# Even and odd columns apart in a two-layer Winograd convolution block, with positions 1 and 3 by columns in three chunks of layer two, and another issue order

## The chip, the cores and the metric

The kernel runs on one core of one Trainium2 chip. The metric is the device time of one execution in microseconds (us); less is better. The median before is that of three runs.

## What is computed

The kernel is a residual block of a diffusion model on two images of 512 channels and 64 x 64 points, in bf16. Each of two layers normalizes in four groups of 128 channels, applies SiLU, and convolves 3 x 3. An embedding is added between the layers, and the input at the end.

```python
B, C, HW, E = 2, 512, 64, 1152
def reference(x, t_emb, g1, be1, w1, w_emb, g2, be2, w2):
    ...
    h = conv3(_silu(gn(x, g1, be1)), w1)
    emb = _silu(t_emb) @ w_emb
    h = h + emb.reshape(B, C, 1, 1)
    h = conv3(_silu(gn(h, g2, be2)), w2)
    return x + h
```

## The kernel before

**Tiling.** The 512 channels are four blocks of 128 partitions: `ct` counts those of the input, `ot` those of the output. Each image is cut into two chunks of 32 rows, so each layer has four chunks (`chunks`, index `idx`). A chunk's rows form eight tiles (`TR`) of four output rows (`TH`).

**Winograd over rows.** Four output rows of three taps need six products in place of twelve, the positions 0 to 5. `u_blocks` turns the weights (transposed by TensorE, L392, and copied out of PSUM, L505) into six weight sets U; `v_block` turns the activated rows into six row sets V. A position is then a plain one-dimensional convolution over columns: three taps `kx`, each a product of 128 x 128 weights with 8 rows x 64 columns = 512 columns, read from a row of 66 elements (`WP`, with one zero at each end) at offset 0, 1 or 2. For four `ct` that makes 12 products, accumulated in one half of an accumulator of two PSUM banks; there are three accumulators (`next_acc`). All these products are issued by `groups` (L655); `row_pair` does two positions.

**The same over columns.** Where `is_col` holds (layer one's chunks 1 to 3, all of layer two), positions 0 and 5 use a second such step over pairs of columns: four products of 256 columns (`c` = 0 to 3) in place of three of 512, in `col_pair`. Products 0 and 3 read every second element of a difference, products 1 and 2 a sum and a difference that lie side by side; the last lines of `make_v` write these. In the last two chunks of layer two positions 1 and 3 go by columns as well: `u_more` makes their weights, `v_more_split` (chunk three) and `v_more` (chunk four) their V, `more_cols` and `more_pair` their products and sums.

**Sums.** `one_set` does one `ot` of one chunk: its accumulators are read by ScalarE (`act`, L353), added on VectorE (`tt`, L323; `stt`, L336; `ts`, L328) and written into an output buffer `yst`. Column results land with stride two, at even and odd columns. In layer one the result goes to `h_scr` in DRAM; in layer two the input is added by a DMA on GpSimd's queue, and a DMA writes the output. `final_set` does the very last `ot`.

**Buffers.** `v_block` loads rows of x or h into `src[i]`, SiLU writes them to `a_tmp[i]` with zeroed edges (GpSimd), and `make_v` works through `vt` into V; `i` alternates between 0 and 1. `Vbuf` holds V of two chunks: that of chunk `idx + 2` overwrites that of chunk `idx` when its products are done.

**Start.** All of the first image is loaded; `first_stats` gets the sums of squares by products of each 128 x 128 block with itself (L955), and plain sums by products with ones (L969) or by ScalarE and VectorE (`SUMS`). `norm` makes scale and shift from them on TensorE, VectorE and GpSimd.

**Order.** Everything is a node of `_Plan` with an engine, an estimated cost, and what it reads and writes. `issue` makes the order of each engine's instructions in a model of the core; it tries 100 variations (`PASSES`), each with noise on all priorities, and keeps the best model time. That order is written out as it is; nothing is reordered behind it.

Of the kernel before, what the change touches and what calls it, by code (L numbers as in the profile page):

```python
# [12 lines left out]
ALU = mybir.AluOpType  # L13
# [11 lines left out]
class _Plan:  # L25
# [5 lines left out]
    PASSES = 100  # L31
    JUSTIFY = 2
# [110 lines left out]
    def issue(self):  # L143
# [23 lines left out]
        rng = random.Random(1)  # L167
        late = backward([-d for d in due])
        best = None
        for k in range(self.PASSES):  # L170
            if best is None:
                trial = late
            else:
                noise = self.NOISE * math.exp(rng.gauss(0.0, 1.0))
                trial = [t + noise * rng.gauss(0.0, 1.0) for t in best[1]]
            found = None
            for r in range(self.JUSTIFY + 1):
                order, start, span = forward(trial)
                if found is None or span < found[0]:
                    found = (span, trial, order, start)  # L180
                if r < self.JUSTIFY:
                    trial = backward([-b - c for b, c in zip(start, self.cost)])
            if best is None or found[0] <= best[0]:
                best = found
            self.spans = getattr(self, "spans", []) + [best[0]]
        _, _, order, start = best
# [6 lines left out]
def kernel(  # L193
# [39 lines left out]
    DVE_SUMS = (1,)  # L233
    COL0 = (1, 2, 3)
# [15 lines left out]
    SUMS = (0, 3)  # L250
# [30 lines left out]
    gparm = mb[0:4 * CT, 0, 0, 0:P]  # L281
# [118 lines left out]
    def norm(layer, b, c0, n, me, ps=None, quick=False):  # L400
# [5 lines left out]
        def mm():  # L406
# [5 lines left out]
        plan.add("DVE", 0.1, lambda: nc.vector.tensor_copy(out=tot[:], in_=ps if ps is not None else bank.get()[:]),  # L412
                 tok if ps is None else [ps], [tot[:]])
# [11 lines left out]
        quick = quick or (layer, b) == (1, B - 1)  # L425
        two(nvar[:], mu, mu, ALU.mult, quick)
        two(nvar[:], nvar[:], ex, ALU.add, quick)
        if quick:
            ts(nvar[:], nvar[:], 0.0, op=ALU.min, c2=-1.0, op1=ALU.mult)
        else:  # L430
# [6 lines left out]
             cost=0.7)  # L437
# [3 lines left out]
        two(nb, mu, sc, ALU.mult, quick)  # L441
        two(nb, nb, b_, ALU.add, quick)
# [90 lines left out]
    more_buf = lambda ct: (a_tmp + src)[ct]  # L533

    def v_more(V, X):
        rows = lambda kx, st: view(V, kx, [[2 * NI, 2], [WP, TR], [st, W // st]])
        dst = lambda o, n: view(X, o, [[n * TR, 2], [n, TR], [1, n]])
        tt(dst(0, W), rows(0, 1), rows(2, 1), ALU.subtract)
        tt(dst(4 * NC, W // 2), rows(1, 2), rows(2, 2), ALU.add)
        tt(dst(6 * NC, W // 2), rows(2, 2), rows(1, 2), ALU.subtract)  # L540

    spare = lambda ct: (stage + [g1t])[ct]

    def v_more_split(V, at, D):
        rows = lambda kx, st: view(at, kx, [[NI, 2], [WP, TR], [st, W // st]])
        tt(view(D, 0, [[W * TR, 2], [W, TR], [1, W]]), rows(0, 1), rows(2, 1), ALU.subtract)
        dst = lambda i: view(V, i * 2 * NI, [[NC, 2], [W // 2, TR], [1, W // 2]])
        tt(dst(0), rows(1, 2), rows(2, 2), ALU.add)
        tt(dst(1), rows(2, 2), rows(1, 2), ALU.subtract)

    def rhs_more_split(V, D, j, c):
        if c in (0, 3):
            return view(D, j * 2 * NC + (1 if c == 3 else 0), [[W, TR], [2, W // 2]])
        return view(V, (c - 1) * 2 * NI + j * NC, [[1, NC]])

# [3 lines left out]
    def rhs_row(V, pos, kx, col):  # L559
        i = pos - 1 if col else pos  # L560
        return view(V, i * NI + kx, [[WP, TR], [1, W]])

    def rhs_col(V, j, c, o=4 * NI):
        if c in (0, 3):
            return view(V, o + j * 2 * NC + (1 if c == 3 else 0), [[W, TR], [2, W // 2]])
        return view(V, o + (4 if c == 1 else 6) * NC + j * NC, [[1, NC]])

    def silu_rows(layer, b, ch, ct, res, at):
# [3 lines left out]
        for edge, r in ((ch == 0, 0), (ch == NCH - 1, CR + 1)):  # L572
            if edge:
                pool(lambda r=r: nc.gpsimd.memset(rows[:, r, 1:W + 1], 0.0), [], [rows[:, r, 1:W + 1]], cost=0.2)  # L574
        act(rows[:, lo - r0:hi - r0, 1:W + 1], res[:, lo * W:hi * W].rearrange("p (r w) -> p r w", w=W)
            if res.shape[1] == HW else res.rearrange("p (r w) -> p r w", w=W),
            func=ACT.Silu, bias=nb_all[layer, b][:, ct:ct + 1], scale=sc_all[layer, b][:, ct:ct + 1])

    def make_v(V, at, rs, col, on_act, split=False):
# [25 lines left out]
        if split:  # L605
# [4 lines left out]
        tt(view(V, o, [[W, 2 * TR], [1, W]]), view(vt_, vo, [[WP, 2 * TR], [1, W]]),  # L610
           view(vt_, vo + 2, [[WP, 2 * TR], [1, W]]), ALU.subtract)
        odd = view(vt_, vo + 1, [[WP, 2 * TR], [2, W // 2]])
        evn = view(vt_, vo + 2, [[WP, 2 * TR], [2, W // 2]])
        tt(view(V, o + 4 * NC, [[W // 2, 2 * TR], [1, W // 2]]), odd, evn, ALU.add)
        tt(view(V, o + 6 * NC, [[W // 2, 2 * TR], [1, W // 2]]), evn, odd, ALU.subtract)

    def v_block(layer, b, ch, ct, V, res=None, rs=None, on_act=(False, True, True)):
        at = a_tmp[count["v"] % 2]
        k = src[count["v"] % 2]
# [9 lines left out]
        split = layer == 1 and b * NCH + ch == len(chunks) - 2  # L629
        make_v(V, at, rs if rs is not None else k, is_col(layer, b, ch), (layer == 1,) + on_act[1:], split)  # L630
        if split:
            v_more_split(V, at, spare(ct))
# [14 lines left out]
    def groups(pos_rhs, accs, gid, lead=0.0):  # L647
        done = {}
        for key, ap, lhs, rhs_, cost in pos_rhs:
            clock["t"] += cost  # L650

            def emit(key=key, ap=ap, lhs=lhs, rhs_=rhs_):
                for l, r in zip(lhs, rhs_):
                    k = done.get(key, 0)
                    nc.tensor.matmul(ap, lhsT=l, rhs=r, start=k == 0, stop=k == total[key] - 1)  # L655
                    done[key] = k + 1
            plan.add("PE", cost, emit, list(lhs) + list(rhs_), [ap], group=("g", gid), lat=0.17, due=clock["t"], lead=lead)
# [8 lines left out]
    def row_pair(pair, U, V, col, gid, split):  # L666
        a = next_acc()
        todo = []
        for i, pos in enumerate(pair):
            for ct in range(CT):  # L670
                taps = [(u_tap(U[ct], pos, kx), rhs_row(V[ct], pos, kx, col)) for kx in range(NKX)]
                todo.append((i, a[:, i], [t[0] for t in taps], [t[1] for t in taps], 0.218 * NKX))
# [3 lines left out]
    def col_pair(cc, U, V, gid, lead=0.0, js=(0, 1)):  # L676
        a = next_acc()
        a4 = a[:].rearrange("p j (k n) -> p j k n", k=2)
        todo = []
        for j in js:  # L680
            for k, c in enumerate(cc):
                pairs = [(u_col(U[ct], j, c), rhs_col(V[ct], j, c)) for ct in range(CT)]
                todo.append(((j, k), a4[:, j, k], [t[0] for t in pairs], [t[1] for t in pairs], 0.11 * CT))
# [3 lines left out]
    def more_cols(U, V, gid):  # L687
        def cols(cc):
            a = next_acc()
            a4 = a[:].rearrange("p j (k n) -> p j k n", k=2)  # L690
            todo = []
            for j in range(2):
                for k, c in enumerate(cc):
                    pairs = [(u_col_more(U[ct], j, c), rhs_more_split(V[ct], spare(ct), j, c)) for ct in range(CT)]
                    todo.append(((j, k), a4[:, j, k], [t[0] for t in pairs], [t[1] for t in pairs], 0.11 * CT))
            groups(todo, a, (gid, "more", cc))
            return a4
        act(mb[:].rearrange("p k j n -> p j k n"), cols((1, 2)), scale=0.5 * KAPPA)
        tt(sd[:, 0], mb[:, 0], mb[:, 1], ALU.add)
        tt(sd[:, 1], mb[:, 0], mb[:, 1], ALU.subtract)  # L700
        aa = cols((0, 3))
        for k, f in ((0, KAPPA), (1, -KAPPA)):
            stt(view(m1, k, [[NFREE, 2], [2, NC]]), aa[:, :, k], f, sd[:, k], ALU.mult, ALU.add)

    def more_set(j, U, gid):
        a = next_acc()
        todo = []
        for k, c in enumerate((0, 3, 1, 2)):
            pairs = [(u_col_more(U[ct], j, c), rhs_col(more_buf(ct), j, c, 0)) for ct in range(CT)]
            todo.append((k, a[:, k // 2, (k % 2) * NC:(k % 2 + 1) * NC], [t[0] for t in pairs],  # L710
                         [t[1] for t in pairs], 0.11 * CT))
# [10 lines left out]
    def more_pair(U, gid):  # L722
        for j in range(2):
            a = more_set(j, U, gid)
# [3 lines left out]
        par = lambda i: view(stage[0], i * 2 * NC, [[NC, 2], [1, NC]])  # L728
        out = lambda i: view(m1, i, [[NFREE, 2], [2, NC]])
        tt(par(0), comp(2), comp(3), ALU.add)  # L730
        tt(par(1), comp(2), comp(3), ALU.subtract)
        tt(out(0), par(0), comp(0), ALU.add)
        tt(out(1), par(1), comp(1), ALU.subtract)

    def final_set(U, V):
# [6 lines left out]
        more_pair(U, gid)  # L742
        a = col_pair((1, 2), U, V, gid, 10.0)
        act(mb[:].rearrange("p k j n -> p j k n"), a, scale=0.5)
        tt(sd[:, 0], mb[:, 0], mb[:, 1], ALU.add)
        tt(sd[:, 1], mb[:, 0], mb[:, 1], ALU.subtract)
        n = CR * W // 2
        y12, y03 = y4[:, 1:3], y4[:, 0:TH:TH - 1]
        both = lambda t, o: view(t, o, [[0, 2], [W, TR], [1, W]])
        tt(y12, y12, both(m1, 0), ALU.add)  # L750
        tt(y03, y03, both(m1, 0), ALU.add)
        for i in range(2):
            sd4 = sd[:, i].rearrange("p j (t w) -> p j t w", t=TR)
            tt(sd4, sd4, view(y, i, [[(TH - 1) * W, 2], [TH * W, TR], [2, W // 2]]), ALU.add)
        z = view(stage[1], 0, [[NFREE, 2], [1, NFREE]])
        e = view(stage[2], 0, [[NFREE, 2], [1, NFREE]])
# [7 lines left out]
        tt(y12, y12, t4(z), ALU.add)  # L764
        a = row_pair((2,), U, V, True, gid, 1)
        q = [view(vt, i * NFREE, [[1, NFREE]]) for i in range(3)]
        act(q[1], a[:, 0], scale=KAPPA)
        act(q[0], a[:, 0], scale=-KAPPA)
        act(q[2], a[:, 0], scale=-KAPPA)
        pm = lambda i: view(vt, i * NFREE, [[NFREE, 2], [1, NFREE]])  # L770
        tt(e, e, pm(1), ALU.add)
        tt(y12, y12, t4(pm(0)), ALU.add)
        aa = col_pair((0, 3), U, V, gid)
        for h in range(2):
            for k, op in ((0, ALU.add), (1, ALU.subtract)):
                part = lambda t: t.rearrange("p j (t w) -> p j t w", t=TR)[:, :, h * TR // 2:(h + 1) * TR // 2]
                tt(view(y, k + h * n, [[(TH - 1) * W, 2], [TH * W, TR // 2], [2, W // 2]]), part(sd[:, k]),
                   part(aa[:, :, k]), op)
            o = view(y, h * n, [[(TH - 1) * W, 2], [TH * W, TR // 2], [1, W]])
# [304 lines left out]
```

## Time and profile before

| | |
|---|---|
| Median of three runs | 500.41 us (499.71 to 500.93) |
| The profiled execution, its own time | 501.14 us |
| Its span, first to last instruction | 499.3 us |
| Mean granted TensorE clock | 0.991 |
| DMA | 55.53 MB, mean 111 GB/s |

The profile names engines PE (TensorE), PEld (TensorE's weight loads), DVE (VectorE), ACT (ScalarE), POOL (GpSimd) and SP (the queue that issues most DMAs). A group of instructions has a line of the kernel, which is often a helper's, the tiles it writes and reads, its shapes and count, then busy us, mean ns of one, and the idle time before. A stretch has its limits and length, busy us and instructions of each engine, the granted clock, and the DMAs' share and GB/s. TensorE's products overlap, so how long one holds the array is read from a dense stretch and its count, not from the mean of one.

### The profile page before, as it was taken

The numbers are of one execution on the slowest core, as the hardware profiler recorded it, in microseconds if no ns is written. First come the engines' busy times: TensorE is split into PE (matmuls) and PEld (weight loads), VectorE is DVE, ScalarE is ACT, GpSimd is POOL, SyncE is SP. The second block draws the span as 40 slices with busy tenths as digits, with TensorE's granted clock in tenths as the row PEclk, the third lists the DMA queues.
The fourth block names the chain that finished last, engine by engine and source line by source line (L and its number), as shares of the span: only waits on it lengthen the run. The fifth ranks groups of instructions, "written<-read, shape, count | busy, mean of one in ns | idle before, by whom it ended". The sixth has DMA issues, their size and how long they took to land. (4 is left out here: it accounts for less than half of the span.)

```text
span 499.3 us, 8442 instructions
## 1 busy us (share of the span) xinstructions
PE 482.5 (97%) x3126; PEld 289.0 (58%) x3128; DVE 465.4 (93%) x996; ACT 399.6 (80%) x548; POOL 57.4 (11%) x130
## 2 busy tenths in 40 slices
PE   7898999999999999999999999999999999999993
PEld 6665544455554555555566565555555667667762
DVE  4889989999999999999999999999999999998666
ACT  4888999999987799999999999767678785635452
POOL 2120000024650004000000001200000000000010
PEclk9999999999999999999999999999999999999997
DMA  8533231551120333224454213424543753243434
GB/s 310 196 75 99 86 117 67 204 200 42 45 85 1 121 95 110 88 85 132 136 164 129 69 44 90 106 80 114 152 103 83 213 129 85 50 120 85 127 85 126
DMA packets 17315, 55.53 MB, mean 111 GB/s; under 512 B 1915, under 2 KB 3067, under 8 KB 16507
## 3 DMA queue, kind: packets, MB, share of 16 engines
q1 hardware_dynamic: 14912, 46.86, 27.4%
q0 software_dynamic: 2160, 7.87, 9.6%
q8 instruction: 24, 0.39, 0.3%
q10 hardware_dynamic: 203, 0.27, 0.1%
q14 instruction: 16, 0.13, 0.1%
HBM read 38.22 MB, written 16.78 MB: 110 GB/s over the span
## 5 line engine op out<-in xcount | busy, mean ns | idle before, releaser
L655 PE MATMUL acc<-V,U 128*128 128x512 bf16 (+1 forms) x2400 | 434.0, 338 | 3.5 <-DVE V L323 1.6
L655 PEld LDWEIGHTS <-U 128*128 128x128 bf16 x2592 | 250.3, 98 | 182.7 <-issue 6.1
L323 DVE TENSOR_TENSOR V<-vt 128x1056 bf16<-128x1056 bf16 (+2 forms) x132 | 89.7, 693 | 0.9
L353 ACT ACTIVATE mb<-acc 128x1024 bf16<-128x1024 f32 x32 | 32.6, 1020 | 21.4 <-PE acc L655 17.4
L353 ACT ACTIVATE w<-acc 128x1024 bf16<-128x1024 f32 (+1 forms) x32 | 32.3, 1008 | 19.9 <-PE acc L655 11.3
L323 DVE TENSOR_TENSOR U<-U 128x768 bf16<-128x768 bf16 (+2 forms) x96 | 45.0, 485 | 1.4 <-ACT U L353 1.2
L353 ACT ACTIVATE m<-w 128x512 bf16<-128x512 bf16 x62 | 37.4, 625 | 10.0 <-DVE w L323 9.9
L323 DVE TENSOR_TENSOR w<-m,w 128x1024 bf16<-128x1024 bf16 (+1 forms) x63 | 43.0, 682 | 1.8 <-ACT w L353 1.1
L353 ACT ACTIVATE a_tmp<-src,arena 128x2112 bf16<-128x2112 bf16 x20 | 42.9, 2144 | 0.9 <-DVE arena L323 0.9
L353 ACT ACTIVATE src<-vt 128x528 bf16<-128x528 bf16 x54 | 34.0, 640 | 9.8 <-DVE vt L323 9.5
L323 DVE TENSOR_TENSOR vt<-a_tmp 128x1056 bf16<-128x1056 bf16 x56 | 38.7, 702 | 2.1 <-ACT a_tmp L353 1.8
L392 PEld LDWEIGHTS <-stage 128*128 128x128 bf16 x288 | 25.4, 143 | 9.2 <-issue 0.8
L353 ACT ACTIVATE y<-y 128x2048 bf16<-128x2048 bf16 x16 | 30.6, 1911 | 0.0
L371 POOL DMA_DIRECT2D y<-in_x_dram x15 | 13.3, 884 | 150.1 <-DVE y L323 120.7
L574 POOL MEMSET a_tmp<- 128x64 bf16 x32 | 5.5, 171 | 217.9 <-DVE vt L323 168.8
L353 ACT ACTIVATE a_tmp<-V,arena 128x2112 bf16<-128x2112 bf16 x12 | 25.8, 2151 | 5.6 <-POOL arena L423 2.8
L323 DVE TENSOR_TENSOR y<-sd,acc 128x512 bf16<-128x512 bf16 (+1 forms) x34 | 23.0, 691 | 5.2 <-PE acc L655 4.9
L323 DVE TENSOR_TENSOR sd<-mb 128x512 bf16<-128x512 bf16 x64 | 26.0, 418 | 1.6 <-ACT mb L353 1.6
L505 ACT COPY U<-xa 128x768 bf16<-128x768 bf16 x31 | 24.9, 803 | 2.4 <-PE xa L392 2.3
L353 ACT ACTIVATE m<-acc 128x1024 bf16<-128x1024 f32 x24 | 24.4, 1018 | 1.9 <-DVE y L323 1.3
L323 DVE TENSOR_TENSOR y<-m,w 128x1024 bf16<-128x1024 bf16 x31 | 21.3, 686 | 2.7 <-ACT m L353 2.5
L323 DVE TENSOR_TENSOR vt<-vt,a_tmp 128x1056 bf16<-128x1056 bf16 x32 | 22.5, 703 | 0.5 <-ACT vt L353 0.4
(121 smaller groups left out, 523.9 us busy)
## 6 DMA issues: line engine op xcount, KB each, us to landing
stage<-in_w_dram SPq DMA_DIRECT2D x32, 288.0 KB, 2.9
src<-h_scr SPq DMA_DIRECT2D x16, 528.0 KB, 3.8
h_scr<-y SPq DMA_DIRECT2D x16, 512.0 KB, 2.8
y<-in_x_dram POOLq DMA_DIRECT2D x15, 512.0 KB, 5.4
out_dram<-y SPq DMA_DIRECT2D x15, 512.0 KB, 2.8
V<-in_x_dram SPq DMA_DIRECT2D x6, 1024.0 KB, 8.2
src<-in_x_dram SPq DMA_DIRECT2D x4, 528.0 KB, 4.1
V<-in_x_dram SPq DMA_DIRECT2D x4, 512.0 KB, 6.6
```

The lines of the kernel that those rows point to most:

```text
L323: lambda: nc.vector.tensor_tensor(out=out, in0=in0, in1=in1, op=op), [in0, in1], [out], **kw)
L353: nc.scalar.activation(out=out, in_=in_, func=fn, scale=scale, **extra)
L371: q.dma_start(out=out, in_=in_, **extra)
L392: nc.tensor.transpose(sel(t), in_, ident[:in_.shape[0], :in_.shape[0]])
L505: lambda: nc.scalar.copy(out=out, in_=sel(bank.get())), [tok], [out])
L574: pool(lambda r=r: nc.gpsimd.memset(rows[:, r, 1:W + 1], 0.0), [], [rows[:, r, 1:W + 1]], cost=0.2)
L655: nc.tensor.matmul(ap, lhsT=l, rhs=r, start=k == 0, stop=k == total[key] - 1)
```

## The change

In every row of an activated chunk the even and the odd columns are now apart: 33 elements (`HP`) of one kind, then 33 of the other. SiLU writes them so. Layer one's result is kept in that form in `h_scr`; layer two's final additions put the columns back in order. A plain tap's 512 columns are then two runs of 32 in each row. The first and the last product of a position are issued as one product over both halves, the other ten as two products of 256 columns each. Column products and their V are read and written side by side.

Positions 1 and 3 go by columns in layer two's chunks 2 to 4 (`FIRST_MORE`), with `v_more` gone and its V made by `v_more_split`; for that space is taken from `a_tmp[1]` and `src[1]` in every second chunk, and `v_block` uses `a_tmp[0]` and `src[0]` alone in layer two's last two chunks. `first_stats` gets plain sums from products with one column of ones; parameters of layer two are loaded later; small steps of `norm` are fused. The order comes from a fixed list of seeds, each a noise on the priorities that fall in one window of time.

```diff
-    PASSES = 100
-    JUSTIFY = 2
+    STEPS = ((0, 3), (300001, 3), (300002, 3), (300003, 3), (300004, 2), (300008, 2), (300011, 3), (300013, 1),
...
+        for seed, rounds in self.STEPS:
+            if seed:
+                rng = random.Random(seed)
                 noise = self.NOISE * math.exp(rng.gauss(0.0, 1.0))
...
+                lo = 520 * rng.random() - 20
+                hi = lo + 10 * math.exp(4 * rng.random())
+                trial = [t + noise * rng.gauss(0.0, 1.0) if lo <= t < hi else t for t in trial]
...
+    FIRST_MORE = 1
...
+    def spare(idx, ct):
+        if idx % 2:
+            return (stage + [g1t])[ct]
+        return view((a_tmp[1], src[1])[ct // 2], ct % 2 * 4 * NC, [[1, 4 * NC]])
 
     def v_more_split(V, at, D):
...
+        pairs = lambda o: view(at, o, [[WP, 2 * TR], [HP, 2], [1, HW2]])
+        tt(view(D, 0, [[W, 2 * TR], [HW2, 2], [1, HW2]]), pairs(0), pairs(1), ALU.subtract)
+        dst = lambda i: view(V, i * 2 * NI, [[HW2, 2 * TR], [1, HW2]])
+        tt(dst(0), halves(at, HP, 2 * TR), halves(at, 1, 2 * TR), ALU.add)
+        tt(dst(1), halves(at, 1, 2 * TR), halves(at, HP, 2 * TR), ALU.subtract)
...
+    HW2 = W // 2
+    HP = WP // 2
+
+    def halves(t, o, rows):
+        return view(t, o, [[WP, rows], [1, HW2]])
...
     def rhs_row(V, pos, kx, col):
         i = pos - 1 if col else pos
-        return view(V, i * NI + kx, [[WP, TR], [1, W]])
+        return [halves(V, i * NI + o, TR) for o in ((0, HP), (HP, 1), (1, HP + 1))[kx]]
+
+    def both_halves(half):
+        step = half[1].offset - half[0].offset
+        return bass.AP(half[0].tensor, half[0].offset, [list(d) for d in half[0].ap[:2]] + [[step, 2], [1, HW2]])
 
     def rhs_col(V, j, c, o=4 * NI):
         if c in (0, 3):
-            return view(V, o + j * 2 * NC + (1 if c == 3 else 0), [[W, TR], [2, W // 2]])
+            return view(V, o + j * 2 * NC + (HW2 if c == 3 else 0), [[W, TR], [1, HW2]])
...
+        first = lo * W if res.shape[1] == HW else 0
+        order = (HW2, [-HW2, 2], [1, HW2]) if layer == 1 else (1, [-1, 2], [2, HW2])
...
-        tt(view(V, o, [[W, 2 * TR], [1, W]]), view(vt_, vo, [[WP, 2 * TR], [1, W]]),
-           view(vt_, vo + 2, [[WP, 2 * TR], [1, W]]), ALU.subtract)
-        odd = view(vt_, vo + 1, [[WP, 2 * TR], [2, W // 2]])
-        evn = view(vt_, vo + 2, [[WP, 2 * TR], [2, W // 2]])
...
+        pairs = lambda i: view(vt_, vo + i, [[WP, 2 * TR], [HP, 2], [1, HW2]])
+        tt(view(V, o, [[W, 2 * TR], [HW2, 2], [1, HW2]]), pairs(0), pairs(1), ALU.subtract)
+        odd, evn = halves(vt_, vo + HP, 2 * TR), halves(vt_, vo + 1, 2 * TR)
...
     def v_block(layer, b, ch, ct, V, res=None, rs=None, on_act=(False, True, True)):
-        at = a_tmp[count["v"] % 2]
-        k = src[count["v"] % 2]
+        one = layer == 1 and b * NCH + ch >= 2
+        at, k = (a_tmp[0], src[0]) if one else (a_tmp[count["v"] % 2], src[count["v"] % 2])
...
-        split = layer == 1 and b * NCH + ch == len(chunks) - 2
+        split = layer == 1 and b * NCH + ch >= FIRST_MORE
...
-                    nc.tensor.matmul(ap, lhsT=l, rhs=r, start=k == 0, stop=k == total[key] - 1)
+                    edge = k in (0, total[key] - 1)
+                    for o, i in [(both_halves(ap), both_halves(r))] if edge and len(r) > 1 else zip(ap, r):
+                        nc.tensor.matmul(o, lhsT=l, rhs=i, start=k == 0, stop=k == total[key] - 1)
...
+    def sums(b):
+        tt(by_cols(sd, 0), by_rows(b[:, 0]), by_rows(b[:, 1]), ALU.add)
+        tt(by_cols(sd, 1), by_rows(b[:, 0]), by_rows(b[:, 1]), ALU.subtract)
...
         aa = cols((0, 3))
         for k, f in ((0, KAPPA), (1, -KAPPA)):
-            stt(view(m1, k, [[NFREE, 2], [2, NC]]), aa[:, :, k], f, sd[:, k], ALU.mult, ALU.add)
...
+            act(by_cols(m1, k), aa[:, k].rearrange("p (j t w) -> p j t w", j=2, w=HW2), scale=f)
+        flat = lambda t: view(t, 0, [[1, 2 * NFREE]])
+        tt(flat(m1), flat(m1), flat(sd), ALU.add)
...
+            tt(t4(m1[:]), t4(m1[:]), s1t1, ALU.add)
+            for f in range(2):
+                act(view(yst, (1 + f) * W, [[TH * W, TR], [1, 2], [2, HW2]]),
+                    m1[:, f].rearrange("p (t k w) -> p t k w", k=2, w=HW2))
...
+                for j, blk in enumerate(blks):
+                    nc.tensor.matmul(cs, lhsT=blk, rhs=ones_bf[:, 0:1], start=(k == 0 and j == 0),
+                                     stop=(k == 1 and j == 15))
...
+    late = [sc_all[0, 0][:, CT - 1:CT]]
+    load_parms(1, (g2, be2), late)
...
-                if layer == 1 and idx == len(chunks) - 3:
+                if layer == 1 and idx == 0:
                     for c0 in range(0, CT, 2):
                         u_more(1, ot, c0, 2)
...
-                    if layer == 1 and nn == len(chunks) - 1:
-                        for ct in range(CT):
-                            v_more(Vs[ct], more_buf(ct))
```

In `final_set` the two additions behind each pair of last sums are gone; what they added is put into `sd` before.

## The prediction

> **What bounds the kernel now.** I read the page's busy times first, then the groups kept apart by shape, then busy times by stretch, the waits of TensorE, and the chain that ended last.
>
> ```profile
> span 499.3 us, 8442 instructions
> PE 482.5 (97%) x3126; PEld 289.0 (58%) x3128; DVE 465.4 (93%) x996; ACT 399.6 (80%) x548; POOL 57.4 (11%) x130
> ```
>
> The groups by shape (busy us, mean ns, idle time before them):
>
> ```profile
> L655 PE MATMUL acc<-V,U 128*128 128x512 bf16 x1440 | 336.3, 382 | 3.3 <-DVE V L323 1.6 <-ACT mb L353 1.4
> L655 PEld LDWEIGHTS <-U 128*128 128x128 bf16 x2592 | 250.3, 98 | 182.7 <-issue 6.1
> ```
>
> TensorE is nearly never free, and each of its 2592 products in `groups` loads its own weights. How long a product occupies the array is read from dense stretches of line 655. The three stretches below hold 66 plain taps (512 columns), 16 column products that read side by side, and 16 that read every second element (the seventeenth in each count is a neighbour that reaches in).
>
> ```profile
> 65.60:79.98 14.38, 14.38 (x66) 6.35 (x66) 1.00 0.15 46
> 108.82:110.55 1.73, 1.73 (x17) 1.56 (x16) 1.00 0.00 0
> 115.94:117.74 1.80, 1.80 (x17) 1.53 (x17) 1.00 0.00 0
> ```
>
> 14.38/66 = 218.0 ns a tap; 1.74/16 = 109.1 ns; 1.81/16 = 113.3 ns. The stretch of taps, asked by tile, shows two kinds:
>
> ```profile
> L655 PE MATMUL acc<-V,U x66: 376/379/386, 65.6 to 79.8; 128*128 128x512 bf16 x66
> ```
>
> Two of three taps take 379 ns, the third (`kx` = 1, whose eight rows begin at an odd element) 386. So an aligned tap holds the array 215.7 ns and the odd one 222.7: 7 ns for eight odd beginnings.
>
> VectorE is the second bound. Layer two's four chunks lie at about 278-335, 335-392, 392-442 and 442-491 us:
>
> ```profile
> 280.00:336.00 56.00, 56.00 (x340) 32.06 (x338) 55.67 (x125) 49.14 (x64) 4.37 (x8) 1.00 0.28 77
> 336.00:392.00 56.00, 56.00 (x323) 31.19 (x322) 55.85 (x104) 39.40 (x46) 4.93 (x9) 1.00 0.48 124
> 392.00:441.00 49.00, 48.74 (x341) 32.88 (x339) 48.83 (x89) 33.45 (x40) 3.78 (x6) 1.00 0.46 112
> 441.00:491.00 50.00, 50.00 (x364) 35.05 (x362) 39.02 (x71) 24.25 (x39) 3.45 (x4) 1.00 0.43 103
> ```
>
> In the first three both engines (first and third busy column) are full. TensorE waits little for anyone, the longest of its waits on line 655 (total, times, longest) being the first row here; the chain (start, length) ends in one long run of TensorE and then VectorE's last additions.
>
> ```profile
> PE acc L655 <- DVE V L323: 1.6, 3, 0.7
> ```
>
> ```profile
> 420.67 58.42 PE acc L655 x408
> ...
> 493.83 1.38 DVE y L323 x3
> 495.23 0.43 DVE y L323
> ```
>
> The sum is made against the profiled execution: 501.14 us, of which the span is 499.3; the three timed runs have their median 0.7 lower.
>
> **TensorE, part by part.** (a) Positions 1 and 3 of layer two's second chunk go by columns: 4 output blocks x 24 taps = 96 taps fewer (96 x 0.218 = 20.9 us), 4 x 32 = 128 products of 256 more (128 x 0.1091 = 14.0): -7.0.
> (b) With the columns apart, the 576 products (half of 1152) that read every second element read runs of 32: 576 x (113.3 - 109.1) = -2.4. [...]
> (c) The other 1344 taps are 112 groups of 12. In each the first and last product stay whole, ten are split: 2240 halves. Unhindered, two halves cost 218.2, against 215.7 or 222.7. But a row is now 33 even and 33 odd elements, so a half begins at offset 0, 33, 1 or 34: of the six halves of three taps four begin odd (0 and 33, 33 and 1, 1 and 34). Let an odd half cost p more. A group costs now 8 x 215.7 + 4 x 222.7 = 2616; then 10 x 218.2 + 14p + 2 x (215.7 + p) = 2613 + 16p. No row shows p. If the 7 ns goes with the elements read, p is 3.5; if with each beginning, 7; if a new instruction absorbs it, 0. The nearest row of the same length is the product with stride two, 4.2 above the plain one, even though half of those begin odd: I take p = 4.2. That is 64 ns a group, +7.2 us; the ends are -0.3 and +12.2.
> TensorE together: -7.0 - 2.4 + 7.2 = -2.2 (from -9.7 to +2.8). The 1152 additional weight loads lie under 109 ns products, as in the second stretch.
>
> **VectorE.** The rows that price it:
>
> ```profile
> L323 DVE TENSOR_TENSOR V<-vt 128x512 bf16<-128x512 bf16 x48 | 32.2, 684 | 0.1
> L323 DVE TENSOR_TENSOR sd<-mb 128x512 bf16<-128x512 bf16 x64 | 26.0, 418 | 1.6 <-ACT mb L353 1.6
> L323 DVE TENSOR_TENSOR V<-vt 128x1024 bf16<-128x1024 bf16 x24 | 16.4, 684 | 0.0
> ```
>
> 512 elements at stride two cost what 1024 side by side cost; beginnings follow each other after 0.60, 0.60 and 0.34 us. So every `v_block` by columns saves 2 x 0.26 = 0.52: 12 blocks in layer one (-6.3), 16 in layer two (-8.3). The additional column form of `v_more_split` costs 0.60 + 2 x 0.34 = 1.28 in 12 blocks in place of 1.80 in 8: +1.0. `more_cols` puts 0.68 + 0.60 = 1.28 on VectorE: +5.1 in chunk two, and -2.8 in chunk three, where it was 0.68 + 2 x 0.65; the two outputs of `more_pair` fall from 0.6 to 0.34 each: -2 in chunk four. The rest of the sums in `one_set` keeps its length.
> All this gains only where VectorE holds TensorE up. Chunk one of layer two gets +3.0 (1.28 x 4 - 2.1), chunk two 5.1 - 4.2 = +0.9, chunk three -7.0; `u_more` moves a chunk earlier. Over the three: 160.4 - 3.1 = 157 us of VectorE, beside 161 - 7 = 154 of TensorE before (c). Some preparation of U can move ahead of 280, where layer one's savings make room. I charge +1.5 (0 to 6).
> ScalarE gets two copies of 512 (0.58 each, from `m<-w` in pairs of 1.15) in 15 sets, +17, and 4 x 0.6 x 4 = +10 in chunks two and three. It has 7 to 16 us free per chunk in the last three; only the first, 49.1 of 56, is near its edge with +5.
>
> **Head, gaps, tail.** TensorE is idle 5.4 us before 25, 1.7 in 25-50 and 1.5 in 100-160. In the head ScalarE's sums (1.9 + 1.1, twice) and VectorE's (1.2, twice) go; 32 one-column products for each block of x come, bounded by nothing below and by the 62 ns of a gram product above, 2 us a block, in place of 1.9 for two blocks; the loads of layer two's parameters, three issues of some 0.4 us on ScalarE's queue, now wait there for the fourth norm; behind them stands the fourth SiLU, which needs that norm anyhow, so I charge nothing (at most 1.2). Shorter norms save about 0.5. With a searched order I take -3.5 for all gaps (0 to -6). Behind the last product, two additions of 0.43 leave the chain: -0.9.
>
> **Sum:** 501.1 - 2.2 + 1.5 - 3.5 - 0.9 = 496.0.
>
> **Rivals.** *Odd beginnings cost nothing in a half (p = 0).* For it: an odd stride-two product costs no more than an even one. Against: the 386 ns row. TensorE falls by 9.7, VectorE then binds layer two for 3 in place of 1.5: 501.1 - 9.7 + 3.0 - 3.5 - 0.9 = 490.0.
> *Slower: one buffer for V.* From chunk three of layer two on, `v_block` uses only `a_tmp[0]` and `src[0]`; now two blocks alternate. The next load waits until the V operations have read `src[0]`. One block alone: load 3.8 (median to landing of `src<-h_scr`), SiLU 2.14, ScalarE 1.08 + 3 x 0.64, VectorE 0.62 between them and 3 x 0.62 + 1.28 behind, some 0.8 for hand-overs: 13.5 us. Queued behind them on VectorE stand the sums of the current set, which hold the accumulators that TensorE needs next; on POOL's queue the zeroing of `a_tmp[0]`'s edge rows now waits for the block before, and the additions of x into the output wait behind that. Four blocks must fit in a chunk of 49 us, with a lead of about 10 for the first; it decides once a block passes 15 us. In the trace blocks under way two at a time take 15 to 25 us from SiLU to last V. At 18 us a block: 3.1 + 3 x 18 = 57, 8 late, of which about 3 are covered by products of the other blocks; twice, 10 us: 506.
> *p = 7 and nothing else:* 501.1 + 2.8 + 1.5 - 3.5 - 0.9 = 501.0, no change.
> *VectorE loses pairs on rows that begin odd.* The 1024 subtraction would take 1.12 (twice 0.60 less the fixed 0.08 that 0.60 and 0.34 show) in place of 0.60 and the 512 ones stay at 0.60: 28 x 1.05 + 12 x 1.05 = +42 on a full engine, about 530 with slack spent. No odd row with step one on VectorE is in this trace, so it speaks neither way. [...]
>
> **Chances.** Forecast 0.42 (493 to 499); p = 0 0.22; one buffer 0.22; no change 0.08; pairs lost 0.06. A measurement of this kernel tells about 0.2% (1 us) from nothing. Faster: 0.36 + 0.21 = 0.57; within 0.2% 0.07; slower 0.36 (one buffer and pairs 0.28, the poor ends of the others 0.08). The range leaves out pairs lost, the far end of one buffer and a little below: 488 to 508.
>
> **What would show it.** Halves at 109 and 113 ns in turn mean p = 4.2; 109 alone p = 0; 116 p = 7. The V operations of 512 elements at 420 ns and the 1024 ones still at 684 mean that pairs are kept. TensorE waiting for V at the start of layer two's last two chunks means one buffer. If plain halves exceed 120 ns, the forecast falls.

## The result, and the profile after

| | before | after |
|---|---|---|
| Median, same chip | 500.29 us (4 runs) | 505.88 us (4 runs, 505.04 to 507.49) |
| Ratio | | 1.0108, 95% interval 1.0085 to 1.0131 |
| Profiled execution, its span | 501.14, 499.3 us | 505.79, 504.0 us |
| Mean granted TensorE clock | 0.991 | 0.996 |

The change made the kernel 1.1% slower. The forecast was 496.0, faster; 505.9 lies inside the range of 488 to 508, towards its upper end.

The head of the page after the change:

```profile
span 504.0 us, 11103 instructions
PE 489.2 (97%) x4393; PEld 397.4 (79%) x4393; DVE 456.4 (91%) x1023; ACT 421.0 (84%) x583; POOL 45.3 (9%) x106
```

VectorE is 9 us less busy than before and TensorE 6.7 us more. The groups kept apart by shape (busy us, mean ns, idle before); `groups` now has line 672, `tt` 322, `act` 352:

```profile
L672 PE MATMUL acc<-V,U 128*128 128x256 bf16 x3328 | 423.4, 276 | 0.7 <-DVE V L322 0.6
L672 PEld LDWEIGHTS <-U 128*128 128x128 bf16 x3744 | 359.0, 97 | 90.5 <-issue 3.3
L672 PE MATMUL acc<-V,U 128*128 128x512 bf16 x224 | 82.8, 384 | 1.8 <-ACT mb L352 1.8
```

1344 plain taps have become 224 whole ones and 2240 halves; 1088 column products stand beside the halves in the first row. (192 further column products read their operand from `stage`, `g1t`, `a_tmp` or `src` and have rows of their own; their weights are counted in the second row.) The layer-two stretches, in the columns of the earlier ones (limits, length, then busy us and instructions of PE, PEld, DVE, ACT, POOL, the clock, the DMAs):

```profile
280.00:334.00 54.00, 54.00 (x462) 43.27 (x460) 51.02 (x121) 50.42 (x70) 5.77 (x5) 1.00 0.34 95
334.00:388.00 54.00, 52.16 (x444) 42.80 (x442) 53.56 (x109) 43.94 (x55) 4.11 (x8) 1.00 0.43 109
388.00:444.00 56.00, 56.00 (x482) 46.61 (x481) 55.16 (x104) 50.52 (x66) 4.77 (x8) 1.00 0.47 117
444.00:495.00 51.00, 51.00 (x439) 42.30 (x438) 36.15 (x71) 31.51 (x50) 3.45 (x4) 1.00 0.43 104
```

TensorE is full in three of the four and misses 1.8 us in the second; its longest waits in `groups` over the whole execution (total us, times, longest) are

```profile
PE acc L672 <- ACT mb L352: 1.8, 2, 1.2
PE acc L672 <- DVE V L322: 0.6, 1, 0.6
```

So the time was not lost to waiting. It is in the products themselves. A dense stretch of layer one's first chunk holds 32 halves (and a neighbour that reaches in):

```profile
76.56:80.30 3.74, 3.74 (x33) 3.06 (x32) 3.71 (x9) 3.74 (x7) 0.00 (x0) 1.00 0.34 140
```

3.74/32 = 117 ns a half, where a plain product of 256 columns holds the array 109.1. From start to start, over the whole trace (no view prints these; they are taken from the start times of its products), an even half takes 113.7 ns, an odd one 118.8, a whole tap of two runs a row 221.9, and a column product, of whichever kind, 109.1. Weight loads (97 ns) stay under all of these.

A group of twelve taps costs 2 x 221.9 + 6 x 232.5 + 4 x 237.6 = 2789 ns (a tap at `kx` 0 or 2 is an even and an odd half, one at `kx` 1 two odd halves), where it cost 2616: +173 ns, 112 times, is **+19.4 us**. (The mean of all halves in the trace is 117.1 ns, which gives 2786 and +19.0: the figure is good to about 0.5 us.) TensorE's idle time, here and below, is counted from start to start as well, as what a gap between two products has beyond the usual length of the first; what is taken as usual moves a total by about 1 us, and the pages, which count overlapping products as busy, show less. The span rose 4.7: +19.4 for these, -7.0 for the third column chunk, -2.4 for the products that no longer read with stride two, -4.6 for TensorE's idle time (16.2 to 11.6, of which 4.3 in the first 50 us), -0.3 for the tail (8.2 to 7.9 behind the last product's start): +5.1, with -0.4 left over.

Not all of that idle time was waiting. In the execution profiled before the change TensorE's granted clock was 0.50 for 3.4 us:

```profile
22.71:26.12 3.41, 3.39 (x22) 2.56 (x22) 3.26 (x13) 1.88 (x1) 1.35 (x3) 0.50 0.24 79
```

Products of 128 columns began there every 107 ns, and every 56 where the clock was 1.00; counted as above, 1.6 of the 16.2 us are this. The execution profiled after the change shows no such stretch from 5 us on, up to its last 5 us. So 1.6 of the -4.6 came from the clock, and about 3 from the edits and the order.

### The profile page after: what moved, and what is told of

Read it like the earlier page. It is cut to its first block, busy times and chain, and to the rows that moved or that the text cites. A ratio compares the mean times of both kernels' runs of the same rounds, so it can differ in the third digit from the quotient of the medians.

```text
span 504.0 us, 11103 instructions
## 1 busy us (share of the span) xinstructions
PE 489.2 (97%) x4393; PEld 397.4 (79%) x4393; DVE 456.4 (91%) x1023; ACT 421.0 (84%) x583; POOL 45.3 (9%) x106
## 5 line engine op out<-in xcount | busy, mean ns | idle before, releaser
L672 PE MATMUL acc<-V,U 128*128 128x256 bf16 (+1 forms) x3552 | 446.1, 283 | 2.5 <-ACT mb L352 1.8
L672 PEld LDWEIGHTS <-U 128*128 128x128 bf16 x3744 | 359.0, 97 | 90.5 <-issue 3.3
L322 DVE TENSOR_TENSOR V<-vt 128x1056 bf16<-128x1056 bf16 (+2 forms) x100 | 60.6, 620 | 1.9 <-ACT vt L352 0.6
L352 ACT ACTIVATE mb<-acc 128x1024 bf16<-128x1024 f32 x36 | 36.7, 1019 | 18.1 <-PE acc L672 14.6
L322 DVE TENSOR_TENSOR sd<-mb 128x512 bf16<-128x512 bf16 x72 | 28.7, 420 | 7.3 <-ACT mb L352 7.3
L322 DVE TENSOR_TENSOR vt<-a_tmp 128x1056 bf16<-128x1056 bf16 x48 | 33.6, 703 | 1.2 <-ACT a_tmp L352 0.8
L352 ACT ACTIVATE m<-acc 128x1024 bf16<-128x1024 f32 (+1 forms) x36 | 29.0, 828 | 3.1 <-PE acc L672 2.2
L352 ACT ACTIVATE y<-m 128x512 bf16<-128x512 bf16 x30 | 21.6, 770 | 2.2 <-DVE m L322 2.2
L322 DVE TENSOR_TENSOR w<-w 128x1024 bf16<-128x1024 bf16 x31 | 21.3, 686 | 2.2 <-ACT w L352 1.6
L352 ACT ACTIVATE src<-V 128x2048 bf16<-128x2048 bf16 x12 | 22.8, 1901 | 0.0
```

Of the source, the lines that this page charges most:

```text
L322: lambda: nc.vector.tensor_tensor(out=out, in0=in0, in1=in1, op=op), [in0, in1], [out], **kw)
L352: nc.scalar.activation(out=out, in_=in_, func=fn, scale=scale, **extra)
L672: nc.tensor.matmul(o, lhsT=l, rhs=i, start=k == 0, stop=k == total[key] - 1)
```

## The experiments

Theory A: the split taps hold the array longer than the sum allowed, and that alone turns the gain into a loss. Rivals: the searched order fits the chip badly; one buffer for V delays the later chunks; VectorE or ScalarE holds TensorE up.

**All taps whole, the order kept.** Both halves go as one product with two runs a row, as the change already does for the first and last of a position.

```diff
-                    edge = k in (0, total[key] - 1)
-                    for o, i in [(both_halves(ap), both_halves(r))] if edge and len(r) > 1 else zip(ap, r):
+                    for o, i in [(both_halves(ap), both_halves(r))] if len(r) > 1 else zip(ap, r):
```

> The kernel after, with every plain tap as one product over both halves (16 runs of 32) in place of two of 256; same order of everything else. Theory A (TensorE's products set the time; an interior tap costs 113.7 + 118.8 = 232.5 ns where one half begins odd and 237.6 where both do): a whole tap costs 222 as the first and last ones of a position do now, 229 for kx = 1 if two odd halves simply add, 238 if the step back between its halves costs as well; that is 97 to 61 ns less a position of 12 taps, 112 positions: 495 to 499 us. Theory B (waits set the time: one buffer for V, ScalarE's additional copies, the searched order): the products get shorter and TensorE waits instead, 503 to 506 us.

Measured: 499.44 us, ratio to before 0.9970 (0.9955 to 0.9986), 6.4 us under the change. A tap at `kx` 0 or 2 takes 221.8 ns, one at `kx` 1 235.3: there the odd columns come first, so the reading steps back by 32 elements within each row. The group is 8 x 221.8 + 4 x 235.3 = 2716, or -73 x 112 = -8.2 us against the halves; 1.2 us came back as idle time (11.6 to 12.8), which leaves 7.0 for 6.4 in the spans. The median is just above the 495 to 499 of Theory A and well under the 503 to 506 of the other. The one buffer, the searched order, and the work of VectorE and ScalarE are all as in the change, and the kernel is faster than before. Theory A holds; none of the rivals is needed for the loss.

**The split alone, in the kernel before: two forms of it.** Left and right 32 columns of each row (the runs that the change reads), and upper and lower four rows (runs of 64).

```diff
-                    nc.tensor.matmul(ap, lhsT=l, rhs=r, start=k == 0, stop=k == total[key] - 1)
+                    tap = size(r) == NFREE and 0 < k < total[key] - 1
+                    for h in range(2) if tap else (None,):
+                        o = ap if h is None else view(ap, h * W // 2, [[W, TR], [1, W // 2]])
+                        i = r if h is None else view(r, h * W // 2, [[WP, TR], [1, W // 2]])
+                        nc.tensor.matmul(o, lhsT=l, rhs=i, start=k == 0, stop=k == total[key] - 1)
```

The second form has `h * NC, [[1, NC]]` for the result and `h * TR // 2 * WP, [[WP, TR // 2], [1, W]]` for the operand.

> The kernel before, columns in their natural order, only the ten inner taps of each position issued as two products of 256: the left 32 columns of each row and the right 32. Theory A, with the cost in the short runs (a run of 32 and then a jump): 2 x 113.7 for kx = 0 and 2, 2 x 118.8 for kx = 1: 130 ns more a position, 120 positions, +15.6: 516 us. If jumps cost nothing and only the number of products and odd beginnings count (109.1, and 7 for an odd half): +3.3: 504 us. Theory B says nothing against either, but then this kernel would show TensorE idle.

> The kernel before, the ten inner taps of each position issued as two products of 256, the upper four rows and the lower four, runs of 64 as before. Theory A: the number of products and weight loads alone costs 2.5 ns a tap, 109.1 for an even half and 112.6 for an odd one: 25 ns a position, +3.0: 503.4 us. If the additional 1200 weight loads are what costs, as much as in e2: 510 us or more.

Measured: 511.74 (ratio 1.0215, 1.0191 to 1.0238) and 502.62 (1.0038, 1.0023 to 1.0053). Halves by columns take 113.6 ns when they begin even and 118.7 when odd, those by rows 109.1 and 112.5. So it is not the number of products that costs, nor their weight loads: the same split with runs of 64 is nearly free. Short runs at this row length cost 4.5 ns a product even where each begins even. The first form came 4 us under its expectation because TensorE's idle time shrank from 16.2 to 11.2, 1.6 of it because this execution has no stretch of lower clock; that the rest are waits which the longer products filled is not shown.

**Single patterns, products alone.** 48 products for each pattern, back to back, weights alternating.

```python
    for n in range(N):  # pitch 66, runs of 32, beginning at an even element
        nc.tensor.matmul(view(acc[n % 2], 0, [[64, 8], [1, 32]]), lhsT=w(n), rhs=view(xs[1], 0, [[66, 8], [1, 32]]), start=True, stop=True)
```

> Products alone, the convolution left out: 64 products to warm up and then 25 ways of reading the moving operand, 48 products each, all in one stream; the time of a product is read from the stream. [...] Theory A2 (the scattered result is what costs): the rows with the result written side by side are 109 and 114, the reversed one is the slowest.

Each pattern is a stretch from its first start to the next pattern's; its length over 48 is the time of one product. Here 256 side by side, then eight runs of 32 at pitch 66 from element 0 and from element 33, at pitch 64 from element 2, at pitch 68 from element 0, then 512 as eight natural rows of 64, as two runs with step 33, with step -32, and with step +32 and the result written in reversed order:

```profile
23.64:28.88 5.24, 5.24 (x49) 4.70 (x48) 0.00 (x0) 0.00 (x0) 1.00 1.01 427
28.88:34.32 5.44, 5.44 (x50) 4.61 (x48) 0.00 (x0) 0.00 (x0) 1.00 1.02 428
39.79:45.48 5.69, 5.69 (x50) 4.59 (x48) 0.00 (x0) 0.00 (x0) 1.00 0.09 36
73.04:78.44 5.40, 5.40 (x51) 4.60 (x48) 0.00 (x0) 0.00 (x0) 1.00 0.00 0
78.44:83.68 5.24, 5.24 (x51) 4.66 (x49) 0.00 (x0) 0.00 (x0) 1.00 0.00 0
110.57:120.93 10.36, 10.36 (x51) 4.70 (x49) 0.00 (x0) 0.00 (x0) 1.00 0.01 2
131.61:142.29 10.68, 10.68 (x50) 4.70 (x49) 0.00 (x0) 0.00 (x0) 1.00 0.01 2
142.29:153.49 11.20, 11.20 (x49) 4.61 (x48) 0.00 (x0) 0.00 (x0) 1.00 0.00 0
153.49:164.49 11.00, 11.00 (x50) 4.70 (x48) 0.00 (x0) 0.00 (x0) 1.00 0.00 0
```

5.24/48 = 109.2 ns; 5.44/48 = 113.3; 5.69/48 = 118.5; 5.40/48 = 112.5; 5.24/48 = 109.2 again at pitch 68; then 215.8, 222.5, 233.3 and 229.2. With the result packed side by side, the patterns at pitch 66 from elements 0 and 1 take 113.3 and 117.8, and with the result scattered 113.4 and 117.8, so it is the reading that costs, not the scattered writing, and Theory A2, which had 109 and 114 for the packed ones, falls. The kernel's periods are found again with no other engine at work. At pitch 68 runs of 32 take the 109.2 of 256 side by side, so short runs alone do not make the 113.3.

**Whole taps, all read forward.** In a tap at `kx` 1 the even columns are read first, and the result is written in reversed order of the halves.

```diff
-                    for o, i in [(both_halves(ap), both_halves(r))] if edge and len(r) > 1 else zip(ap, r):
+                    for o, i in [(both_halves(q), both_halves(h)) for q, h in [(ap, r) if len(r) < 2 or
+                            r[0].offset < r[1].offset else (ap[::-1], r[::-1])]] if len(r) > 1 else zip(ap, r):
```

> e1 with the middle tap (kx = 1) read forward, its two halves written in reversed order. If the step back in reading is what makes that tap 235 ns: 229, -3 us against e1: 496 us. If writing back to front costs as much: no change, 499. If it costs more: over 500.

Measured: **497.67 us, ratio to before 0.9917 (0.9889 to 0.9946)**, 8.2 us under the change; under the kernel before it is 2.6 us by the median in the first table and 3.8 by the one timed beside it (501.42). `kx` 1 falls from 235.3 to 228.2 ns, the others rise to 222.9: 8 x 222.9 + 4 x 228.2 = 2696, -2.2 us against the version before it; the spans differ by 3.1, of which 1.0 is idle time (12.8 to 11.8).

**The order.** The search of the kernel before (100 variations, noise everywhere) in place of the list of seeds, and then, with that search, positions 1 and 3 by columns in two chunks only.

```diff
-    FIRST_MORE = 1
+    FIRST_MORE = 2
...
-                if layer == 1 and idx == 0:
+                if layer == 1 and idx == FIRST_MORE - 1:
```

> The kernel after, its order made by the search of before (100 variations with noise on everything) in place of the list of seeds. Theory A: the same TensorE work, more idle time, 507 to 512 us. If the list's order is what makes the kernel slow on the chip: below 504 us.

> The kernel of e4 (after, order by the search of before) with positions 1 and 3 by columns in two chunks of layer two as before. TensorE gets 96 split taps for 128 column products: 96 x 233 - 128 x 109 = 8.4 us more; if TensorE sets the time: ratio 1.018 + 0.017 = 1.035, 518 us. If VectorE or the single buffer held layer two up and the third chunk's columns gained nothing: 510 us as e4.

Measured: 510.06 (1.0184, 1.0161 to 1.0208) and 514.57 (1.0265, 1.0233 to 1.0297). With the old search TensorE's idle time is 15.9 us in place of 11.6, 4.9 of it between 300 and 400: the searched order gained 4 us and was no cause of the loss. The first 50 us keep their lower idle time (8.6, against 12.3 before the change), so that gain comes from the edits at the start, but for the 1.6 us of the clock. The third column chunk saves 96 taps at 2789/12 = 232.4 ns for 128 products of 109.1: 8.3 us of TensorE. The medians differ by only 4.5 us, and part of that is the clock: four of the five executions without the third chunk (514.6 to 515.8) had a granted clock of 0.988 to 0.992, all four with it 0.995 to 0.997. In the two profiled executions, both at 0.997, the spans are 510.4 and 508.3, 2.1 us apart (and the two have different orders, since the search runs on each). Without the third chunk TensorE idles 0.1 us between 300 and 450, with it 5.1, waiting for VectorE and ScalarE. So more than half of the gain becomes waits in layer two under this search; under the searched order of the change TensorE idles about 2.6 us there.

**The order and the layout, each searched anew.** First the whole-tap version read forward, with new seeds and a tap told to the order's model at 0.2247 us in place of 0.218. Then all of the change except the layout: columns in natural order, taps whole, stride two in `rhs_col`, `make_v`, `v_more_split` and the sums. The core of the second:

```diff
-        return [halves(V, i * NI + o, TR) for o in ((0, HP), (HP, 1), (1, HP + 1))[kx]]
+        return [view(V, i * NI + kx, [[WP, TR], [1, W]])]
...
-        tt(dst(0), halves(at, HP, 2 * TR), halves(at, 1, 2 * TR), ALU.add)
+        tt(dst(0), rows(1, 2), rows(2, 2), ALU.add)
...
-    by_cols = lambda t, k: view(t, k * HW2, [[NFREE, 2], [W, TR], [1, HW2]])
+    by_cols = lambda t, k: view(t, k, [[NFREE, 2], [W, TR], [2, HW2]])
```

> The whole-tap version with kx = 1 read forward (497.7 us), with a tap told to the order's model at 0.2247 us in place of 0.218 and a new list of seeds searched for it in the same way (windows of local noise, 3,000 seeds). TensorE's work is unchanged, 8 x 222.9 + 4 x 228.2 a group; only its idle time can change: 11.8 us in the version before it, of which 7.3 in the first 50 us and 3.4 between 300 and 450. Theory (products set the time, the order only removes waits): 494 to 498, at best the 3.4 us of the waits in layer two. Rival (the chip's waits are not those that the model sees): no change or up to 3 us slower, 497 to 501.

> All of the change but the layout: columns stay in their natural order (plain taps are one product of 512 at offsets 0, 1, 2, column products 0 and 3 read with stride two, V and the sums of columns are written with stride two by VectorE), positions 1 and 3 by columns in three chunks, the new head, and an order searched anew for it (seeds as in the run beside it). TensorE against the whole-tap version: 112 x (2696 - 2616) = -9.0, column products +2.4: 491 if TensorE alone set the time. VectorE against it: 28 blocks x 0.52 = +14.6, 12 blocks of the second column form x 0.52 = +6.2, and two sums of 0.60 for 0.34 in the sets of layer two; of that some 25 us fall in layer two's first three chunks, where VectorE is busy 160 of 164 us. Theory that the layout pays through VectorE: 500 to 510. Rival that VectorE's room elsewhere takes it up: 491 to 496.

Measured: 501.96 (1.0031, 1.0011 to 1.0051) and 517.17 (1.0322, 1.0286 to 1.0359). The first misses both ranges: the products take what they took, and TensorE idles 18.9 us in place of 11.8, 4.6 of the difference in the first 50 us; 1.8 us of it is a stretch at a granted clock of 0.50 there (20.2 to 23.6 us). Two orders from the same model differ by 4 us on the chip, so the order's own worth is known no better than that, and the 4 us that the searched order gained above are of one pair of orders.

The second is beyond both of its ranges, above 510. It is 15 us slower than the first, although its products are 112 x (2696 - 2616) - 2.4 = 6.6 us shorter. TensorE idles 40.1 us, 23 of them between 300 and 450. The page and the longest waits of TensorE on the accumulators (total us, times, longest):

```profile
PE 483.0 (94%) x3273; PEld 294.3 (57%) x3273; DVE 482.5 (94%) x1022; ACT 403.3 (78%) x553; POOL 46.5 (9%) x106
```

```profile
PE acc L662 <- ACT mb L344: 7.1, 5, 3.3
PE acc L662 <- DVE V L314: 4.6, 4, 3.3
PE acc L662 <- ACT m L344: 2.5, 2, 1.4
```

VectorE has 26 us more to do than with the columns apart. Here are the page of the first version, and the sums into `sd` of the change and of the natural layout:

```profile
PE 484.2 (96%) x3273; PEld 296.8 (59%) x3273; DVE 456.3 (91%) x1023; ACT 419.7 (84%) x583; POOL 44.7 (9%) x106
```

```profile
L322 DVE TENSOR_TENSOR sd<-mb 128x512 bf16<-128x512 bf16 x72 | 28.7, 420 | 7.3 <-ACT mb L352 7.3
L314 DVE TENSOR_TENSOR sd<-mb 128x512 bf16<-128x512 bf16 x72 | 43.7, 633 | 3.8 <-ACT mb L344 3.8
```

But the 15 us are not the price of the layout alone. 48 of these 72 sums write with stride two in the natural version. The kernel before, in the same natural order, writes all of its own side by side (418 ns, in the prediction's rows), and for 30 of them, those of `one_set` in layer two, it does no other work in exchange: at some 0.28 us each, about 8 of the 26 us come from how this version is written. Its granted clock was also 0.50 for 13.6 us, in three stretches, of which this is the longest:

```profile
403.59:410.41 6.82, 5.58 (x27) 3.82 (x27) 6.82 (x12) 4.39 (x5) 0.00 (x0) 0.50 0.28 79
```

A column product took 213 ns there, and in the other two a tap 422 to 432; that makes about 6 of the 40.1 us, against 1.8 of the 18.9. And two orders differ by 4 us. So it is shown that this natural version has VectorE full and TensorE waiting, and not what the layout is worth. The best kernel in natural order on record is the one before, at 500.3; the best with columns apart took 497.7, so all of the change with its best taps is worth 0.8%. By the whole-tap runs, what cost the change its gain was the form in which the taps read the layout.

## Why the prediction was wrong, point by point

**(c), the split taps: the step that failed.** The sum took 2613 + 16p ns for a group with p = 4.2: +7.2 us, at most +12.2. It measured 2789, +19.4. What had no reason in the sum was the price of the even half; the formula had two gaps. It set an even half at 109.1, as if runs of 32 at pitch 66 cost what 256 side by side cost; it is 113.7. Twenty halves a group, 4.6 ns each, are 92 of the 109 ns by which a group passed 2680. The other was size: an odd half costs 5.1 more than an even one, not 4.2 (14 x 0.9 = 13 ns), and a whole tap of two runs 221.9, not 219.9 (4 ns). No row priced the even half, and no upper end was given for it. The product with stride two, from which the prediction took p, would have given the even half by its number (the single patterns take 113.4 in both forms), but that the two have one cause is not shown: eight runs of 32 at pitch 64 or 68 take 109.1. "If plain halves exceed 120 ns, the forecast falls" was set too high for the same reason: a mean of 117 was enough.

**(a) and (b): right in TensorE's work.** The column products at 109.1 give -7.0 and -2.4. (The prediction's quotients do not come out as written, 1.74/16 being 108.8 and 1.81/16 113.1; from start to start the trace before has 109.1 and 113.7.) How much of (a) reaches the time was seen above, under the old search: at equal clock about a quarter of what it saves TensorE there. On (b), the same products fell from 113.7 to 109.1 ns when their stride of two went.

**Weight loads: right.** 97 ns each, under halves of 114 to 119.

**VectorE: pairs are kept, rival refuted.** Pairs is the prediction's name for what its rows show: 1024 elements side by side took VectorE as long as 512 at stride two (684 ns each). Whether that also holds for rows that begin odd, it left open:

```profile
L322 DVE TENSOR_TENSOR V<-vt 128x512 bf16<-128x512 bf16 x32 | 13.4, 433 | 0.1
...
L322 DVE TENSOR_TENSOR V<-vt 128x1024 bf16<-128x1024 bf16 x16 | 11.5, 719 | 0.2 <-PE acc L672 0.2
```

The 512 form, all of whose rows of input now begin odd, fell from 684 to 433 ns, close to the 420 of sums that begin even. The 1024 form, half of whose runs now begin odd, rose from 684 to 719, where the loss of pairs was to add some 520. So these operations stayed near the times of even rows; where the 35 ns come from is not shown. The charge of +1.5 for VectorE in layer two is near the 2.5 us of idle time between 300 and 400 in size, but the waits named there end with ScalarE's reading of an accumulator (the 1.8 us above), so it is not shown that VectorE caused them. ScalarE's copies into the natural order are longer than plain ones:

```profile
L352 ACT ACTIVATE m<-w 128x512 bf16<-128x512 bf16 x62 | 37.1, 623 | 2.7 <-DVE w L322 2.3
L352 ACT ACTIVATE y<-m 128x512 bf16<-128x512 bf16 x30 | 21.6, 770 | 2.2 <-DVE m L322 2.2
```

A pair of them lasts about 1.40 us, where the prediction reckoned with 1.15: 15 x 0.25 = 3.8 us more on ScalarE.

**Gaps, start and tail:** -4.6 for +1.5 - 3.5 together, -0.3 for -0.9. Of the -4.6, 1.6 is luck: the stretch of lower clock in the execution that the sum started from, which the prediction did not consider.

**The rival "one buffer for V", 506: the right time by the wrong mechanism.** TensorE waits for V 0.6 us once, and not in layer two, where the rival would have it. With that one buffer kept, whole taps bring the kernel under the time before. Giving the second buffer back was not tried: its place holds the third column chunk's V. **"p = 0"** fell with the periods. **"p = 7 and nothing else"** had the odd half nearly right (118.8 for 116) but not the even one.

That 505.9 lies inside the range is luck too: the range reached up there for the one buffer, and the sum's own worst case for the taps ended at 501.0. With the measured group in place of the assumed one, the prediction's own sum is 496.0 + 19.4 - 7.2 = 508.2; better gaps than charged, with the smaller gain at the tail (-2.6 + 0.6), bring it to 506.2, against 505.8 for the profiled execution.

## What to carry to other kernels

When a layout is changed for one engine, price what every other reader of it then does, and price the shape of the reading (run length, pitch, beginning), not the number of columns: here 5 to 10 ns in each of 2240 products outweighed 9.4 us of TensorE's work and 9 of VectorE's that the change saved. Where no row of the trace shows the new shape, its plainest case needs an upper end too, and not only what is added for the odd one. The way out can be small: the same data read as one product with two runs in rising order gave 497.7 us where two products gave 505.9. Work taken from a bound engine is worth its length only as far as the next engine has room: of 8.3 us that the third column chunk took from TensorE, 2.1 were left at equal clock, under one search. And before a few us are put down to an edit, compare the granted clock of the two executions: one stretch of 3.4 us at half clock was worth 1.6 us here.

## What the runs showed of the hardware

Times of one product (128 x 128 weights, bf16), by how the moving operand (`rhs`, here the activations) is read, from the single patterns, as the mean from start to start:

| columns, pattern | even beginning | odd beginning |
|---|---|---|
| 256 side by side | 109.2 | |
| 256 at stride two | 113.4 | |
| 256, 4 runs of 64, pitch 66 | 109.2 | 112.5 |
| 256, 8 runs of 32, pitch 66 | 113.4 | 117.8 (at 1), 118.7 (at 33) |
| 256, 8 runs of 32, pitch 64 | 109.1 (at 0), 112.5 (at 2) | 116.0 |
| 256, 8 runs of 32, pitch 68 | 109.1 | |
| 256, 8 runs of 32, pitch 72 | 109.2 | 116.1 |
| 512, 8 rows of 64, pitch 66 | 215.8 | 222.5 |
| 512, two runs a row, pitch 66, step 33 | 222.5 | |
| 512, two runs a row, pitch 66, step -32 | | 233.4 |
| 512, the same, step +32, result reversed | | 229.1 |
| 512, two runs a row, pitch 68, step 34 | 215.9 | 229.2 |

Eight runs of 32 from an even beginning cost 4.2 ns at pitch 66 and nothing at pitch 68. Two runs a row cost 6.7 ns at pitch 66 with step 33 and nothing at pitch 68 with step 34. Odd beginnings cost 4 to 7 ns more in eight runs of 32. Reading a `kx` = 1 tap forward and writing it in reversed order is cheaper than the reverse (229.1 against 233.4; in the kernels 228.2 against 235.3). These rows give no simple rule: half of the runs at pitch 66 from element 0 begin at a multiple of four elements and the product takes 113.4, none of those at pitch 64 from element 2 do and it takes 112.5, and of the sixteen runs at pitch 68 with step 34 half do, and they cost nothing. Why stays open. Where the granted clock was 0.50, products began about half as often: those of 128 columns every 107 ns (56 at 1.00), of 256 every 213, of 512 every 422 to 432.
